# Known mean for layer norm 2, token halves for the first gate/up chunks, late roots on Pool, and a new order of the inverse stage

**Chip, cores, metric.** One core of one Trainium2 chip. The metric is the device time in microseconds (us); the kernel before took 492.64 us (median of 3, 492.58 to 492.88).

## The reference

One transformer-like block over `x` of 2048 tokens by 576 columns, in bfloat16 with float32 inside:

```python
h  = x + irfft2(rfft2(layernorm(x)) * (w_r + 1j*w_i))          # spectral filter
h2 = h + (gelu(layernorm(h) @ w_gate) * (layernorm(h) @ w_up)) @ w_down   # 576 -> 4608 -> 576
```

`layernorm(x)` has mean zero in every token, so the column-frequency-zero part of its spectrum is zero and the filter adds nothing to a token's mean: the mean of `h` is the mean of `x`. The change rests on that.

## The kernel before

Tokens lie in 16 tiles of 128. After the forward transforms, an *inverse stage* makes `h` for tiles 0 to 7, normalises and turns tiles 0 to 3, and then the *body* starts: for each of four blocks of 512 tokens, 36 chunks of gate and up matmuls (two parts each), then the down matmuls. Tiles 8 to 15 are made by deferred inverse work inside the first down phase. The stage's order is written as a string: `I` and `N` are the two inverse matmul steps of a tile, `s` its sum of squares (ScalarE), `m`, `r` statistics (VectorE), `q` square root (ScalarE), `c` reciprocal (VectorE), `n` the normalisation (VectorE; `p` on Pool), `A`, `D`, `z` the turn (a transposition) on TensorE with eviction, the copy out of PSUM, by ScalarE, VectorE or both. In the profiles XO holds the tokens, GS the copy of an `I` result (by ScalarE, on VectorE too for tile 0), HN a normalised tile, HT its turned form, WG and WD the weights. The lines of the code that matter here (`...` marks what is left out):

```python
QR = ((0, 2), (2, 4), (4, NPRE), (NPRE, 16))          # tiles that share one root
SEQ = """I0 I1 N0 I2 s0 N1 I3 N2 m0 s1 I4 r0 q0 s2 N3 c0 m1 s3 n1 n0 r1 I5 q1 N4 I6 A1 c1 n3 A0 n2 N5 I7 D2 z3 N6 N7"""
...
    def st_N(c):                                       # residual add, and the token sums on the side
        ... v.scalar_tensor_tensor(x2, banks(SLOT["N", c], 2, 288), 1.0, x2, op0=ALU.mult, op1=ALU.add,
                                   accum_out=SB2[:, 0, c:c + 1])
    def square(c, out, key):                           # sum of squares
        ... a.activation(out, XO[:, c, 0:D], ACTF.Square, accum_out=SB2[:, 1, c:c + 1])
    def ln2_m(q):  # mean = -sum/D; mean^2             VectorE, two instructions
    def ln2_r(q):  # var = sumsq/D - mean^2            VectorE
    def ln2_q(q):  # sqrt(var + eps)                   ScalarE
    def ln2_c(q):  # 1/sqrt                            VectorE
    def norm(c, eng=DVE):                              # (x - mean) * rs, 576 columns + a repeated 64
...
    for tb in range(4):
        for f in range(36):
            gu_part(36 * tb + f, False)
            if f:
                gu_part(36 * tb + f - 1, True)
            ...
            if tb == 0 and f == 8:
                ln2_m(2); ln2_r(2); ln2_q(2); ln2_c(2)     # tiles 4 to 7
            ...
        if tb == 0:
            ln2_m(3); ln2_r(3); ln2_q(3); ln2_c(3)         # tiles 8 to 15
```

## Time and profile before

| | before |
|---|---|
| traced span | 491.0 us |
| stage start to first gate/up matmul | 48.36 to 60.94, 12.58 us |
| useful TensorE work in it | 10.94 us |
| body, one block: gate/up, down | 70.04, 35.39 us |

The table's second row is the distance from the first `I` matmul of the inverse stage to the first gate/up matmul, both as the chain of waits gives them. The lines are in the prediction.

### The profile page before, as it was taken

What the parts mean: (1) busy time and instruction counts of PE and PEld (TensorE: products, weight loads), DVE (VectorE), ACT (ScalarE), POOL (GpSimd) and SP (SyncE); (2) the same over time, 40 slices, a digit from 0 to 9 for tenths busy, and PEclk for the clock granted to TensorE, in tenths of its full rate; (3) what the DMA queues carried; (4) which work ended last, traced back from release to release, by engine and by line L of the source; (5) the groups of instructions that cost most, each with busy time, mean ns of one, the idle gap of its engine ahead of it and who ended that gap; (6) DMA issues with size and microseconds to landing.
All of it is one profiled execution on the core that took longest, in us unless ns stands there. A gap on an engine that the chain in (4) does not pass through costs nothing.

```text
span 491.0 us, 9838 instructions
## 1 busy us (share of the span) xinstructions
PE 484.6 (99%) x4337; PEld 289.4 (59%) x4338; DVE 195.1 (40%) x416; ACT 155.5 (32%) x296; POOL 24.8 (5%) x41
## 2 busy tenths in 40 slices
PE   7999999999999999999999999999999999999998
PEld 3787655555688844444577644444677544444775
DVE  6999833443456534333311143433211233333111
ACT  6899845323221252232200023223100122333000
POOL 6211601000000010000000000000000000000000
PEclk9999999999999999999999999999999999999999
DMA  8980997210000071100000001000000000000000
GB/s 290 250 309 16 371 365 258 86 28 20 1 13 19 13 232 24 23 3 1 1 19 13 19 16 26 15 1 1 7 19 18 8 2 1 1 1 1 13 19 19
DMA packets 25147, 31.26 MB, mean 64 GB/s; under 512 B 11440, under 2 KB 17840, under 8 KB 25104
## 3 DMA queue, kind: packets, MB, share of 16 engines
q1 hardware_dynamic: 22208, 18.68, 13.0%
q0 software_dynamic: 2896, 11.95, 6.8%
q8 instruction: 34, 0.56, 0.5%
q14 instruction: 9, 0.07, 0.1%
HBM read 26.29 MB, written 2.36 MB: 58 GB/s over the span
## 4 chain that ended last, share of the span: by engine, by line
PE 95%; DVE 2%; DMA 1%; SPq 0%; issue 0%; POOL 0%; DVEq 0%; POOLq 0%
PE PS L841 57%; PE PS L891 29%; PE PS L586 2%; PE PS L596 2%; PE PS L526 1%; DMA XO<-in_A_x_dram 1%; PE PS L626 1%; PE PS L858 1%; PE PS L701 1%; PE PS L740 1%; DVE ST L470 1%; DVE XO L743 0%; PE PS L872 0%; SPq L219 0%; DVE HN L774 0%
## 5 line engine op out<-in xcount | busy, mean ns | idle before, releaser
L841 PE MATMUL PS<-HT,WG 64*128 64x512 bf16 x2106 | 228.5, 376 | 0.0
L841 PEld LDWEIGHTS PS<-HT,WG 64*128 64x128 bf16 x2106 | 107.6, 94 | 119.5 <-issue 1.0
L851 DVE TENSOR_TENSOR AT<-GL,PS 128x512 bf16<-128x512 bf16 x144 | 99.0, 688 | 174.8 <-ACT GL L850 174.8
L850 ACT ACTIVATE GL<-PS 128x512 bf16<-128x512 f32 x144 | 85.9, 597 | 257.2 <-PE PS L841 243.6
L891 PE MATMUL PS<-WD,AT 128*128 128x288 bf16 (+2 forms) x1152 | 144.3, 286 | 0.0
L891 PEld LDWEIGHTS PS<-WD,AT 128*128 128x128 bf16 x1152 | 110.8, 98 | 30.7 <-ACT GL L850 1.3
L894 DVE TENSOR_TENSOR OS<-PS,XO 128x288 bf16<-128x288 f32 (+2 forms) x32 | 14.7, 458 | 100.3 <-PE PS L891 100.3
L841 PE MATMUL PS<-HT,WGX 64*128 64x512 bf16 x486 | 53.4, 376 | 0.0
L841 PEld LDWEIGHTS PS<-HT,WGX 64*128 64x128 bf16 x486 | 23.7, 94 | 28.8
L731 ACT ACTIVATE JD<-XO 128x576 bf16<-128x576 bf16 x8 | 5.5, 683 | 28.5 <-DVE XO L875 28.5
L586 PE MATMUL PS<-FT,U 128*128 128x288 bf16 x96 | 14.2, 286 | 0.0
L605 DVE TENSOR_TENSOR TP<-YS,WS 128x1152 bf16<-128x1152 bf16 (+2 forms) x17 | 11.8, 720 | 0.3
L526 PE MATMUL PS<-ATS,XO 128*128 128x128 bf16 (+1 forms) x128 | 10.1, 221 | 1.3 <-POOL XN L540 0.8
L470 DVE BATCH_NORM_STATS2 ST<-XO 128x6 f32<-128x288 bf16 x24 | 9.3, 439 | 4.1 <-DMA XO<-in_A_x_dram 4.1
L586 PEld LDWEIGHTS PS<-FT,U 128*128 128x128 bf16 x96 | 9.3, 98 | 2.4 <-DVE U L535 0.2
L577 ACT ACTIVATE YS<-PS 128x576 bf16<-128x576 f32 x15 | 9.6, 652 | 2.0 <-PE PS L596 1.8
L774 DVE TENSOR_SCALAR HN<-XO,TM,RS 128x576 bf16<-128x576 bf16 (+1 forms) x32 | 10.0, 363 | 0.0
L596 PE MATMUL PS<-CUS,BT 128*128 128x288 bf16 x64 | 10.0, 286 | 0.0
L526 PEld LDWEIGHTS PS<-ATS,XO 128*128 128x128 bf16 (+1 forms) x128 | 7.5, 97 | 4.0 <-POOL XN L540 1.3
L577 ACT ACTIVATE CUS<-PS 128x576 bf16<-128x576 f32 x14 | 9.1, 651 | 0.8 <-PE PS L586 0.4
L875 DVE SCALAR_TENSOR_TENSOR XO<-PS,XO 128x576 bf16<-128x576 f32 x8 | 6.1, 758 | 8.0 <-PE PS L872 8.0
L626 PE MATMUL PS<-VT,ZS 128*128 128x256 bf16 x64 | 8.8, 273 | 0.3 <-DVE ZS L616 0.3
(79 smaller groups left out, 211.6 us busy)
## 6 DMA issues: line engine op xcount, KB each, us to landing
WD<-in_B_w_down_dram POOLq DMA_DIRECT2D x9, 576.0 KB, 20.8
WG<-in_B_w_up_dram SPq DMA_DIRECT2D x4, 1152.0 KB, 8.1
WG<-in_B_w_gate_dram POOLq DMA_DIRECT2D x4, 1152.0 KB, 10.1
out_dram<-OS SPq DMA_DIRECT2D x30, 72.0 KB, 1.6
XO<-in_A_x_dram SPq DMA_DIRECT2D x3, 576.0 KB, 6.9
WGX<-in_B_w_gate_dram POOLq DMA_DIRECT2D x1, 1152.0 KB, 6.9
WGX<-in_B_w_up_dram SPq DMA_DIRECT2D x1, 1152.0 KB, 10.2
HT<-HN SPq DMA_TRANSPOSE x60, 2.4
```

What stands on the lines that cost most here:

```text
L470: P.op(DVE, lambda v, c=c, h=h: v.bn_stats(ST1[:, c, h, :], XO[:, c, 288 * h:288 * h + 288]), r=[("X", c)], w=[("ST1", c, h)])
L526: P.op(PE, lambda t, b=b, lhs=lhs, p0=p0, p1=p1, s=s, e=e, o=o, c=c: t.matmul(bank(b, p0, p1, o, o + 128), lhs, ATS[:, c, :], start=s, sto ...
L577: fn = (lambda v: v.tensor_copy(dst, src)) if eng == DVE else (lambda a: a.activation(dst, src, ACTF.Copy))
L586: P.op(PE, lambda t, b=b, m=m, us=us, o=o, g=g: t.matmul(bank(b, 0, 128, 0, 2 * HK), U[:, us, g, :, :], FT[:, 3 * o + (2 if us == 4 else u ...
L596: P.op(PE, lambda t, b=b, tb=tb, m=m, s3=s3, sp_=sp_: t.matmul(bank(b, 0, 128, 0, KW), BT[:, sp_, tb, :], CUS[:, s3, m, :], start=(m == 0) ...
L605: P.op(DVE, lambda v: v.tensor_tensor(TP[:, sl, :, :, q0:q1], y4, w4, op=ALU.mult), r=[("Y", sl), ("Wn", i)] + (wkeys[0] if 1 <= g < 9 els ...
L626: P.op(PE, lambda t, b=b[c], c=c, zp=zp, sp_=sp_, z3=z3: t.matmul(bank(b, 0, 128, 256 * c, 256 * c + 256), ZS[:, z3, zp, c:256:2], VT[:, s ...
L841: op = P.op(PE, lambda t, h0=h0, kt=kt, wt=wt, b=b, s=(not second and j == 0), e=(second and j == n - 1): t.matmul(bank(b), wg_tile(slot)[ ...
L850: P.op(ACT, lambda a: a.activation(GL[:, s2, :], bank(b0), ACTF.Gelu_apprx_tanh), r=[("PS", b0)], w=[("GL", s2)])
L851: P.op(DVE, lambda v: v.tensor_tensor(AT[:, f, :], GL[:, s2, :], bank(b0 + 1), op=ALU.mult), r=[("GL", s2), ("PS", b0 + 1)], w=[("AT", f)])
L891: P.op(PE, lambda t, b=b, d0=d0, d1=d1, f=f, p=p: t.matmul(bank(b, 0, 128, 0, d1 - d0), AT[:, f, 128 * p:128 * p + 128], WD[:, f, d0:d1], ...
L894: P.op(DVE, lambda v, b=b, d0=d0, d1=d1, p=p, c=c: v.tensor_tensor(OS[:, p % 2, d0:d1], bank(b, 0, 128, 0, d1 - d0), XO[:, c, d0:d1], op=A ...
```

## The change

Four things at once. (1) The sum of squares is taken around the mean kept from layer norm 1, so the sums, means and mean squares of layer norm 2 go away. (2) The first two chunks run in two token halves, so that the first half needs only tiles 0 and 1 turned. (3) Roots for tiles 4 to 15 become a power of -0.5 on Pool. (4) The stage has a new order, with three of four normalisations on Pool.

```diff
+PARTS = ((0, 256), (256, 512))
-QR = ((0, 2), (2, 4), (4, NPRE), (NPRE, 16))
-SEQ = """I0 I1 N0 I2 s0 N1 I3 N2 m0 s1 I4 r0 q0 s2 N3 c0 m1 s3 n1 n0 r1 I5 q1 N4 I6 A1 c1 n3 A0 n2 N5 I7 D2 z3 N6 N7"""
+QR = ((0, 2), (2, 3), (3, 4), (4, 8), (8, 16))
+SEQ = """I0 I1 N0 I2 s0 N1 I3 s1 N2 I4 q0 s2 c0 N3 I5 s3 p1 q1 N4 q2 I6 N5 c1 c2 p0 A1 I7 n3 N6 A0 z3 N7 p2 D2 G0 G1"""
...
+        P.op(POOL, ... g.tensor_scalar(NM[:, c:c1], src, f, 1.0, ...))        # minus the mean of layer norm 1
-  a.activation(out, XO[:, c, 0:D], ACTF.Square, accum_out=SB2[:, 1, c:c + 1])
+  a.activation(out, XO[:, c, 0:D], ACTF.Square, bias=NM[:, c:c + 1], accum_out=SB2[:, 1, c:c + 1])
-  v.scalar_tensor_tensor(x2, banks(...), 1.0, x2, ..., accum_out=SB2[:, 0, c:c + 1])
+  v.tensor_tensor(x2, banks(...), x2, op=ALU.add)
-  ln2_m, ln2_r
+    def ln2_late(q):
+        P.op(POOL, ... g.tensor_scalar(RS2, SB2[:, 1], 1.0 / D, EPS, op0=ALU.mult, op1=ALU.add))
+        P.op(POOL, ... g.tensor_tensor(RS2, RS2, EXQ, op=ALU.pow))             # EXQ is -0.5
+    def gu_first(i):                                                          # "G0", "G1"
+        for a in range(4):
+            gu_part(a % 2, a > 1, *PARTS[i])
... (PSUM slots of the stage recomputed; deferred work of the first down phase put into a table, same places)
```

More of the change, by code (lines that the diff above doesn't have):

```diff
@@ L28 @@
 DENG, BENG = ['act', 'dve', 'dve', 'act', 'act', 'act', 'act', 'act', 'act', 'act', 'act', 'act', 'act', 'act', 'act', 'act'], ['dve', 'act', 'act', 'act', 'act', 'act', 'act', 'act', 'act', 'act', 'act', 'act', 'act', 'act', 'act', 'act']
-QR = ((0, 2), (2, 4), (4, NPRE), (NPRE, 16))
-SEQ = """I0 I1 N0 I2 s0 N1 I3 N2 m0 s1 I4 r0 q0 s2 N3 c0 m1 s3 n1 n0 r1 I5 q1 N4 I6 A1 c1 n3 A0 n2 N5 I7 D2 z3 N6 N7""".split()
+QR = ((0, 2), (2, 3), (3, 4), (4, 8), (8, 16))
+DSTEP, DLAG = (36, 22) if NPRE == 8 else (28, 22)
+SEQ = """I0 I1 N0 I2 s0 N1 I3 s1 N2 I4 q0 s2 c0 N3 I5 s3 p1 q1 N4 q2 I6 N5 c1 c2 p0 A1 I7 n3 N6 A0 z3 N7 p2 D2 G0 G1""".split()
 def _np_bf16(a):
@@ L355, in _build @@
     EPT = sb.alloc("EPT", [128, 1], F32)
+    EXQ = sb.alloc("EXQ", [128, NT], F32)
+    NM = sb.alloc("NM", [128, NT], F32)
     MK = sb.alloc("MK", [128, 4], F32)
@@ L407, in _build @@
     P.op(POOL, lambda g: g.memset(ZD[:, :], 0.0), w=["ZD"])
+    P.op(POOL, lambda g: g.memset(EXQ[:, :], -0.5), w=["EXQ"])
     P.op(POOL, lambda g: g.memset(MK[:, :], 0.0), w=["MK"])
@@ L548, in _build @@
         RUN1[w[0]](*((int(a[:-1]), ENG[a[-1]]) if a[-1] in ENG else (int(a),)))
+    c = 0
+    while c < NT:
+        c1 = c + 1
+        while c not in ACT_TILES and c1 < NT and c1 not in ACT_TILES:
+            c1 += 1
+        src, f, keys = (SA[:, 0, c:c1], -1.0 / D, "SA0") if c in ACT_TILES else (MV1[:, c:c1, 0], -1.0, "MV1")
+        P.op(POOL, lambda g, c=c, c1=c1, src=src, f=f: g.tensor_scalar(NM[:, c:c1], src, f, 1.0, op0=ALU.mult, op1=ALU.mult),
+             r=[(keys, k) for k in range(c, c1)], w=[("NM", k) for k in range(c, c1)])
+        c = c1
     P.alias([("XN", c) for c in range(NT)], [("V", g, c) for g in range(NG) for c in range(2)])
@@ L690, in _build @@
     vkeys = vk[0] + vk[1] + vk[2]
-    SLOT = {}
-    for w in SEQ:
-        if w[0] in "INADz":
-            SLOT["T" if w[0] in "ADz" else w[0], int(w[1:])] = len(SLOT)
-    SLOT = {k: 2 * ((v - len(SLOT)) % 4) for k, v in SLOT.items()}
+    SLOT, last = {}, [0] * 4
+    smm = [w for w in SEQ if w[0] in "IJNADzG"]
+    g0 = smm.index("G0")
+    for t, w in enumerate(w for w in smm if w[0] != "G"):
+        b = min((2, 3) if t >= g0 - 2 else range(4), key=lambda b: last[b])
+        last[b] = t + 1
+        SLOT["T" if w[0] in "ADz" else "I" if w[0] == "J" else w[0], int(w[1:])] = 2 * b
     def i_mm(c, h, i):
@@ L702, in i_mm, with i_ev @@
                                                               start=(i == 0), stop=(i == 2)), r=vk[i] + ["DT"], w=[("PS", b)])
-    def i_ev(c):
+    def i_ev(c, eng=ACT):
         sl, b0 = c % 2, SLOT["I", c]
@@ L709, in i_ev @@
         else:
-            P.op(ACT, lambda a, sl=sl, b0=b0: a.activation(GS[:, sl, :, 0:KW], banks(b0, 2, KW), ACTF.Copy),
-                 r=[("PS", b0), ("PS", b0 + 1)], w=[("G", sl, 0), ("G", sl, 1)])
+            ev(eng, GS[:, sl, :, 0:KW], banks(b0, 2, KW), [("PS", b0), ("PS", b0 + 1)], [("G", sl, 0), ("G", sl, 1)])
     def st_I01():
@@ L722, in st_I01, with st_I @@
             i_ev(c)
-    def st_I(c):
+    def st_I(c, eng=ACT):
         for h in range(2):
@@ L727, in st_I @@
                 i_mm(c, h, i)
-        i_ev(c)
+        i_ev(c, eng)
     def square(c, out, key):
-        P.op(ACT, lambda a, c=c, out=out: a.activation(out, XO[:, c, 0:D], ACTF.Square, accum_out=SB2[:, 1, c:c + 1]),
-             r=[("X", c)], w=[key, ("S1", c)])
+        P.op(ACT, lambda a, c=c, out=out: a.activation(out, XO[:, c, 0:D], ACTF.Square, bias=NM[:, c:c + 1], accum_out=SB2[:, 1, c:c + 1]),
+             r=[("X", c), ("NM", c)], w=[key, ("S1", c)])
     def st_N(c):
@@ L742, in st_N @@
         x2 = XO[:, c, 0:D].rearrange("p (a b) -> p a b", a=2)
-        P.op(DVE, lambda v, x2=x2, c=c, sl=sl: v.scalar_tensor_tensor(x2, banks(SLOT["N", c], 2, 288), 1.0, x2, op0=ALU.mult, op1=ALU.add,
-                                                               accum_out=SB2[:, 0, c:c + 1]),
-             r=[("PS", SLOT["N", c]), ("PS", SLOT["N", c] + 1)], w=[("X", c), ("S0", c)])
-    def ln2_m(q):
-        c0, c1 = QR[q]
-        P.op(DVE, lambda v, c0=c0, c1=c1: v.tensor_scalar(TM[:, 1, c0:c1], SB2[:, 0, c0:c1], -1.0 / D, None, op0=ALU.mult), r=[("S0", c) for c in range(c0, c1)], w=[("MN", q)])
-        P.op(DVE, lambda v, c0=c0, c1=c1: v.tensor_tensor(TM[:, 0, c0:c1], TM[:, 1, c0:c1], TM[:, 1, c0:c1], op=ALU.mult), r=[("MN", q)], w=[("M2", q)])
-    def ln2_r(q):
-        c0, c1 = QR[q]
-        P.op(DVE, lambda v, c0=c0, c1=c1: v.scalar_tensor_tensor(RS2[:, c0:c1], SB2[:, 1, c0:c1], 1.0 / D, TM[:, 0, c0:c1], op0=ALU.mult, op1=ALU.subtract),
-             r=[("M2", q)] + [("S1", c) for c in range(c0, c1)], w=[("V2", q)])
+        P.op(DVE, lambda v, x2=x2, c=c: v.tensor_tensor(x2, banks(SLOT["N", c], 2, 288), x2, op=ALU.add),
+             r=[("PS", SLOT["N", c]), ("PS", SLOT["N", c] + 1)], w=[("X", c)])
     def ln2_q(q):
         c0, c1 = QR[q]
-        P.op(ACT, lambda a, c0=c0, c1=c1: a.activation(RS2[:, c0:c1], RS2[:, c0:c1], ACTF.Sqrt, bias=EPT[:, 0:1]), r=[("V2", q), "EPT"], w=[("SD2", q)])
+        P.op(ACT, lambda a, c0=c0, c1=c1: a.activation(RS2[:, c0:c1], SB2[:, 1, c0:c1], ACTF.Sqrt, scale=1.0 / D, bias=EPT[:, 0:1]),
+             r=[("S1", c) for c in range(c0, c1)] + ["EPT"], w=[("SD2", q)])
     def ln2_c(q):
@@ L765, in ln2_c @@
         P.op(DVE, lambda v, c0=c0, c1=c1: v.reciprocal(RS2[:, c0:c1], RS2[:, c0:c1]), r=[("SD2", q)], w=[("RS2", q)])
+    def ln2_late(q):
+        c0, c1 = QR[q]
+        P.op(POOL, lambda g: g.tensor_scalar(RS2[:, c0:c1], SB2[:, 1, c0:c1], 1.0 / D, EPS, op0=ALU.mult, op1=ALU.add), r=[("S1", c) for c in range(c0, c1)], w=[("V2", q)])
+        P.op(POOL, lambda g: g.tensor_tensor(RS2[:, c0:c1], RS2[:, c0:c1], EXQ[:, c0:c1], op=ALU.pow), r=["EXQ", ("V2", q)], w=[("RS2", q)])
     def lq(c):
@@ L773, in norm @@
         for i, (o0, o1, x0, x1) in enumerate(((0, D, 0, D), (D, 640, 512, D))):
-            P.op(eng, lambda v, c=c, hs=hs, o0=o0, o1=o1, x0=x0, x1=x1: v.tensor_scalar(HN[:, hs, o0:o1], XO[:, c, x0:x1], TM[:, 1, c:c + 1],
+            P.op(eng, lambda v, c=c, hs=hs, o0=o0, o1=o1, x0=x0, x1=x1: v.tensor_scalar(HN[:, hs, o0:o1], XO[:, c, x0:x1], NM[:, c:c + 1],
                                                                                         RS2[:, c:c + 1], op0=ALU.add, op1=ALU.mult),
-                 r=[("X", c), ("MN", q), ("RS2", q)], w=[("HN", hs, i)])
+                 r=[("X", c), ("NM", c), ("RS2", q)], w=[("HN", hs, i)])
     def turn_dma(c):
@@ L799, in turn_pe, with sq @@
             P.op(e, fn, r=[("PS", b0 + q0 // 512)] + ([("PS", b0 + 1)] if eng else []), w=[("HT", 0, c, k0)])
-    def sq(c):
-        square(c, OS[:, c % 2, :], ("OS", c % 2, 0))
-    RUN = {"I": st_I, "N": st_N, "s": sq, "m": ln2_m, "r": ln2_r, "q": ln2_q, "c": ln2_c, "n": norm, "p": lambda c: norm(c, POOL), "A": lambda c: turn_pe(c, ACT), "D": lambda c: turn_pe(c, DVE),
-           "z": lambda c: turn_pe(c, None)}
-    st_I01()
-    for w in SEQ[2:]:
-        RUN[w[0]](int(w[1:]))
-    P.alias(ukeys + [("CU", a) for a in range(3)], [("WD", j) for j in range(9)])
-    for j in range(9):
-        P.dma(POOL, WD[:, 4 * j:4 * j + 4, :], wdv[:, 4 * j:4 * j + 4, :], f"wd{j}", w=[("WD", j)])
-    P.alias(vkeys, ["EB", "Q0", "Q1", "YB0", "YB1", "JD"])
-    fdead = ["DT", "IT", "J0", "J1", "ZD"] + [(n_, c) for n_ in ("ATB", "ATS") for c in range(NT)] + [("G", 0, 0), ("G", 0, 1), ("G", 1, 0), ("G", 1, 1), ("Y", 0), ("Y", 1)]
-    fdead += [("T", a, h) for a in range(2) for h in range(2)] + [("Z", a) for a in range(NZ)] + [("ZR", a, h) for a in range(2) for h in range(4)]
-    fnew = ([("AT", f) for f in range(36)] + [("GL", 0), ("GL", 1)] + [("HT", 1, i, k) for i in range(4) for k in range(5)])
+    def sq(c, eng=ACT):
+        if eng == ACT:
+            square(c, OS[:, c % 2, :], ("OS", c % 2, 0))
+            return
+        x = XO[:, c, 0:D]
+        P.op(DVE, lambda v: v.scalar_tensor_tensor(OS[:, c % 2, :], x, NM[:, c:c + 1], x, op0=ALU.add, op1=ALU.mult, accum_out=SB2[:, 1, c:c + 1]),
+             r=[("X", c), ("NM", c)], w=[("OS", c % 2, 0), ("S1", c)])
     def fidx(m):
@@ L826, in _build, with gu_part @@
     first_done = {}
-    def gu_part(m, second):
+    def gu_part(m, second, c0=0, c1=512):
         tb, f = m // 36, fidx(m)
@@ L839, in gu_part @@
                 b = 2 * (m % 4) + o
-                aft = [first_done[m, o]] if second and j == 0 else []
+                aft = [first_done[m, o]] if j == 0 and (second or c0) else []
                 op = P.op(PE, lambda t, h0=h0, kt=kt, wt=wt, b=b, s=(not second and j == 0), e=(second and j == n - 1): t.matmul(
-                    bank(b), wg_tile(slot)[h0:h0 + 64, wt, 128 * (f % 9):128 * (f % 9) + 128], HT[h0:h0 + 64, kt, :], start=s, stop=e),
-                    r=[("HT", tb % 2, i, k) for i in range(4) for k in range(5)] + [("WG", slot, i) for i in range(4)],
+                    bank(b, 0, 128, c0, c1), wg_tile(slot)[h0:h0 + 64, wt, 128 * (f % 9):128 * (f % 9) + 128], HT[h0:h0 + 64, kt, c0:c1], start=s, stop=e),
+                    r=[("HT", tb % 2, i, k) for i in range(c0 // 128, c1 // 128) for k in range(5)] + [("WG", slot, i) for i in range(4)],
                     w=[("PS", b)], after=aft)
-                if not second:
-                    first_done[m, o] = op
-        if not second:
+                first_done[m, o] = op
+        if not second or c1 < 512:
             return
@@ L852, in gu_part @@
              r=[("GL", s2), ("PS", b0 + 1)], w=[("AT", f)])
+    def gu_first(i):
+        for a in range(4):
+            gu_part(a % 2, a > 1, *PARTS[i])
+    P.alias([("ATB", c) for c in range(8)], [("AT", 0), ("AT", 1)])
+    RUN = {"I": st_I, "J": lambda c: st_I(c, DVE), "S": lambda c: sq(c, DVE), "N": st_N, "s": sq, "q": ln2_q, "c": ln2_c, "n": norm, "p": lambda c: norm(c, POOL), "A": lambda c: turn_pe(c, ACT), "D": lambda c: turn_pe(c, DVE),
+           "z": lambda c: turn_pe(c, None), "G": gu_first}
+    st_I01()
+    for w in SEQ[2:]:
+        RUN[w[0]](int(w[1:]))
+    P.alias(ukeys + [("CU", a) for a in range(3)], [("WD", j) for j in range(9)])
+    for j in range(9):
+        P.dma(POOL, WD[:, 4 * j:4 * j + 4, :], wdv[:, 4 * j:4 * j + 4, :], f"wd{j}", w=[("WD", j)])
+    P.alias(vkeys, ["EB", "Q0", "Q1", "YB0", "YB1", "JD"])
+    fdead = ["DT", "IT", "J0", "J1", "ZD"] + [(n_, c) for n_ in ("ATB", "ATS") for c in range(NT)] + [("G", 0, 0), ("G", 0, 1), ("G", 1, 0), ("G", 1, 1), ("Y", 0), ("Y", 1)]
+    fdead += [("T", a, h) for a in range(2) for h in range(2)] + [("Z", a) for a in range(NZ)] + [("ZR", a, h) for a in range(2) for h in range(4)]
+    fnew = ([("AT", f) for f in range(2, 36)] + [("GL", 0), ("GL", 1)] + [("HT", 1, i, k) for i in range(4) for k in range(5)])
     def def_i(c):
@@ L874, in def_n, with turn, defer @@
         x2 = XO[:, c, 0:D].rearrange("p (a b) -> p a b", a=2)
-        P.op(DVE, lambda v, x2=x2, c=c: v.scalar_tensor_tensor(x2, banks(4, 2, 288), 1.0, x2, op0=ALU.mult, op1=ALU.add, accum_out=SB2[:, 0, c:c + 1]),
-             r=[("PS", 4), ("PS", 5)], w=[("X", c), ("S0", c)])
+        P.op(DVE, lambda v, x2=x2, c=c: v.tensor_tensor(x2, banks(4, 2, 288), x2, op=ALU.add),
+             r=[("PS", 4), ("PS", 5)], w=[("X", c)])
         square(c, JD[:, :], "JD")
+    def turn(c):
+        norm(c)
+        turn_dma(c)
+    DEF = {}
+    def defer(t, fn, *a):
+        DEF.setdefault(t, []).append(lambda: fn(*a))
+    for j, c in enumerate(range(NPRE, NT)):
+        defer(DSTEP * j, def_i, c)
+        defer(DSTEP * j + DLAG, def_n, c)
+    if NPRE < 8:
+        t2 = DSTEP * (8 - NPRE) + DLAG
+        defer(t2 - 14, ln2_late, 3)
+        for c in range(4, 8):
+            defer(t2 - 2 + DSTEP * (c - 4), turn, c)
     def down(tb, p):
@@ L884, in down @@
             b = (0, 1, 2, 3)[2 * (p % 2) * (tb > 0) + h] if tb or p < 3 else 6 + h
-            cd = NPRE + 2 * p + h if tb == 0 else NT
-            if cd < NT:
-                def_i(cd)
-            for f in [*range(36)] if tb == 0 else [*range(9, 36), *range(9)]:
-                if cd < NT and f == 22:
-                    def_n(cd)
+            for k, f in enumerate([*range(36)] if tb == 0 else [*range(9, 36), *range(9)]):
+                if tb == 0:
+                    for fn in DEF.get(72 * p + 36 * h + k, ()):
+                        fn()
                 P.op(PE, lambda t, b=b, d0=d0, d1=d1, f=f, p=p: t.matmul(bank(b, 0, 128, 0, d1 - d0), AT[:, f, 128 * p:128 * p + 128],
@@ L901, in _build @@
         for f in range(36):
-            gu_part(36 * tb + f, False)
-            if f:
+            if tb or f > 1:
+                gu_part(36 * tb + f, False)
+            if f > 2 or tb and f:
                 gu_part(36 * tb + f - 1, True)
@@ L908, in _build @@
                 sq(4 + f)
-            if tb == 0 and f == 8:
-                ln2_m(2)
-                ln2_r(2)
-                ln2_q(2)
-                ln2_c(2)
+            if tb == 0 and f == 8 and NPRE == 8:
+                ln2_late(3)
             f0, f1 = (15, 3) if tb == 0 else (2, 4)
-            if tb < 3 and f >= f0 and (f - f0) % f1 == 0 and (f - f0) // f1 < 4:
+            if (tb or NPRE == 8) and tb < 3 and f >= f0 and (f - f0) % f1 == 0 and (f - f0) // f1 < 4:
                 norm(4 * (tb + 1) + (f - f0) // f1)
@@ L921, in _build @@
         if tb == 0:
-            ln2_m(3)
-            ln2_r(3)
-            ln2_q(3)
-            ln2_c(3)
+            ln2_late(4)
             P.alias(vkeys + ["DP", "ITD", "EB", "Q0", "Q1", "YB0", "YB1", "JD"], [("WG", 3, k) for k in range(4)])
```

## The prediction

> **What bounds the kernel now.** I read first the chain that ended last, in order of time: it says which engine sets the end, and from when.
>
> ```profile
> 47.35 0.88 DVE VR L641
> 48.23 0.14 issue
> 48.36 1.63 PE PS L701 x12
> ...
> 57.04 0.69 DVE XO L743 x2
> 57.73 0.05 issue
> 57.77 0.66 PE PS L740 x4
> 58.44 0.73 PE PS L701 x6
> 59.17 0.71 PE PS L794 x10
> 59.88 1.02 PE PS L740 x8
> 60.90 0.04 issue
> 60.94 70.11 PE PS L841 x648
> ...
> 172.41 70.04 PE PS L841 x648
> 242.45 35.39 PE PS L891 x288
> ```
>
> Columns: start, length, what. From 60.94 us to the end at 491.0 the chain is TensorE alone, apart from the last 0.4 us: gate and up matmuls (L841), down matmuls (L891) and the deferred inverse between them (41.36 us from 131.05 to 172.41 instead of 35.39). The edit leaves this body as it is but for the first two chunks. So only the start of the body can move: the inverse stage, 48.36 to 60.94, 12.58 us (I matmuls L701, N matmuls L740, turns of the normalised tiles L794).
>
> Second, TensorE's timeline of that stage; the spacing of starts matters, because a matmul's own length (286 ns) overlaps the next.
>
> ```profile
> 55.90 0.29 PE L701 MATMUL PS<-DT,VR 128*128 128x288 bf16 x1
> 56.65 0.91 PE L794 MATMUL PS<-IDT,HN 128*128 128x128 bf16 x10 [0.46 <-DVE HN L774]
> 57.77 0.66 PE L740 MATMUL PS<-GS,IT 128*128 128x288 bf16 x4 [0.21 <-DVE XO L743]
> 59.16 0.72 PE L794 MATMUL PS<-IDT,HN 128*128 128x128 bf16 x10
> 59.74 1.15 PE L740 MATMUL PS<-GS,IT 128*128 128x288 bf16 x8
> 60.94 2.33 PE L841 MATMUL PS<-HT,WG 64*128 64x512 bf16 x20
> ```
>
> Steady spacing is 0.1225 us for a 288-wide matmul (50 from 49.90 to 56.02) and about 0.057 us for a 128-wide turn (ten from 59.16 to 59.74). Work: 80 x 0.1225 + 20 x 0.057 = 10.94 us. The stage lasts 12.58, so TensorE loses 1.64 us: 0.07 before the first N, 0.63 before the first turns (56.02 to 56.65), 0.55 before N5 (57.22 to 57.77), 0.16 at 59.0, 0.22 before L841. This 1.64 us, 0.33% of 492.64, is a ceiling on what a reordering can give.
>
> Third, VectorE and Pool in the same stretch, to see what TensorE waits for.
>
> ```profile
> 53.72 0.48 DVE L751 TENSOR_SCALAR TM<-SB 128x2 f32<-128x2 f32 x1
> 55.79 1.18 DVE L774 TENSOR_SCALAR HN<-XO,TM,RS 128x576 bf16<-128x576 bf16 x4
> 56.95 0.75 DVE L743 SCALAR_TENSOR_TENSOR XO<-PS,XO 128x576 bf16<-128x576 f32 x1
> 59.64 1.16 DVE L798 CAST HT<-PS 128x640 bf16<-128x640 f32 x2
> ```
> ```profile
> 9.43 0.67 POOL L540 TENSOR_SCALAR XN<-XO 128x576 bf16<-128x576 bf16 x1
> 49.71 6.81 POOL L219 DMA_DIRECT2D WD<-in_B_w_down_dram x9
> ```
>
> VectorE runs N-adds, statistics, norms and an eviction in one queue. The N4 add could start at 55.45, when N4's matmuls end, and starts at 56.95 behind statistics and norms; N5 waits for it. L841 starts just after the last turned part leaves PSUM (59.64 + 1.16 = 60.80). Pool only issues the nine WD loads.
>
> **What the Trainium skill says.** "TensorE: Matmul & The Clock Gate", section Back-to-back issue gap, gives N/2.4 + 2.5 ns warm; here 288 columns cost 122.5 ns, which agrees, and a pair of 64-row, 512-wide matmuls 70.04/324 = 216.2 ns, which agrees for two that run side by side. Its section LDWEIGHTS (loading the stationary operand) says a load goes by columns and not by rows: here 94 ns (64 rows) against 98 (128 rows). "SBUF — State Buffer", section Who interferes with whom, says Pool and VectorE's two-port modes lock each other out of a shared port pair; the 128x2 statistics instruction of 0.48 us beside the WD issue, against 0.16 for a 128x4 one at 79.07 with Pool idle, fits. "GPSIMD Engine Reference", section Engine selection, calls one-input work on Pool roughly line rate: the 576-wide XN takes 0.67 us, VectorE's norm 0.43.
>
> **The change part by part.**
>
> *Known mean.* Gone from VectorE in the stage: two L751 (0.48 + 0.31), two L752, two L756 (0.16 each), eight accumulator reads (0.08), together about 2.1 us; added: one more reciprocal, 0.16. Squares now take the mean as bias at the same 0.67 us. The path from the N1 add to a normalised tile shortens to square, root, reciprocal, norm. In the deferred part eight accumulator reads go, beside busy TensorE: worth nothing. Nine tiny Pool instructions (estimated 0.25 us each) make the means after Pool's last XN at 17.1, in a gap that lasts until 24.75: nothing.
>
> *Norms on Pool.* Three of four go there. Estimated from XN: 0.67 for 576 columns, 0.24 for the 64-wide one (864 wide takes 0.91, so 0.83 ns a column on 0.19), about 0.16 between two: 1.2 us a tile. WD issue moves behind them, to about 59 to 66; WD is first read at 131.
>
> *New order.* I placed each instruction with its measured length and queue. N0 to I6 run as before to 56.02, and N5 follows at once: its GS copy ends near 55.9, its bank is free since the N3 add near 55.5. VectorE no longer stands still: N3 add about 54.75, N4 55.5, N5 56.7. ScalarE: root of tiles 0 and 1 at 54.33, reciprocal 54.67 to 54.83. Pool: p1 54.96 to 56.03, p0 to 57.3. TensorE: A1 56.51, I7 56.80, N6 57.6 (0.05 lost for its GS copy), A0 58.08. Reciprocals of tiles 2 and 3 near 57.4, n3 57.65 to 58.25, p2 to 58.75 or 59.0. Then z3 58.37, N7 58.74 (0.09 lost), D2 59.23 to 59.51. Tile 0 leaves PSUM about 59.29, so the first half chunk starts near 59.5 and covers the eviction of D2 (about 60.1 to 60.95). This loses 0.2 instead of 1.64 us. A walk without slips is too good: n3 and p2 want the shared port together, and if Pool wins, z3 and all after it come 0.5 later. I take 59.75 (59.5 to 60.1), a gain of 1.2 us.
>
> *Two token halves.* A chunk has 10 matmuls in its first part and 8 in its second; two chunks are 36 matmuls or 18 pairs of 512 columns, 18 x 216.2 ns = 3.89 us. They become 36 pairs of 256 columns. If streaming binds, 256/2.4 + 2.8 (the surplus of 216.2 over 213.3) = 109.5 ns a pair, 3.94 us; if two loads bind at the 57 ns of a turn with its load, 116 ns, 4.18 us. Cost 0.05 to 0.3, taken as 0.15.
>
> *Roots by Pool.* Four table loads of 1.28 us (78.45, 80.06, 172.33, 174.18) go from ScalarE. TensorE did not wait there (70.11 against 70.04 in the later bodies), so at most 0.07 us. Pool's power has no duration in this trace; for tiles 4 to 7 it has from 78 to the norm at about 91, for the last eight from 172 to 178.
>
> Sum: 1.2 - 0.15 = 1.05 us; 492.64 - 1.05 = 491.6.
>
> **Rivals.** (1) *Pool becomes the wait.* If a norm takes 2 us instead of 1.2, through pointer scalars or lock-out, p2 ends about 61, D2 and the whole body behind it: 492.6 to 493. For: three norms in series on a slow engine in front of D2. Against: the first two have a microsecond of slack. (2) *Weight loads bind in the halves.* At two full 94 ns loads a pair, 36 x 0.188 = 6.8 us, 2.9 more than now: 494.3. Against: turns load 128 columns every 57 ns. (3) *The ceiling is reached*: no port conflict, streaming halves: 60.94 - 59.5 - 0.05 = 1.4, so 491.2. (4) *The power is slow*: at over 6 us the norm of tile 8 blocks VectorE's queue at 178 and gate/up banks fill; a few us lost once. Against: three spare pairs of banks, nearly 6 us of slack.
>
> **Range and chances.** Repeats of before span 0.3 us. The good end is bounded by 1.64; the bad end by rivals 1 and 2, which I hold at one in six together. 491.0 to 492.6. A move of 2% is 9.9 us: six times the idle that exists, and no rival costs it.
>
> **What would show it.** Right: L841 starts at 59.5 to 60.1; 72 matmuls of 64x256 in about 4.0 us; no TensorE wait over 0.3 us after 56; N5 directly behind I6; later bodies still 70.04 and 35.39; ScalarE without root loads after the first body begins. Wrong: a TensorE wait at D2 on Pool's HN, a 256-wide pair over 0.12 us, an L841 start past 60.6, or the first body longer than 70.2 past its halves because VectorE waits for Pool's power.

## The result, and the profile after

| | before | changed |
|---|---|---|
| time, first comparison | 492.76 us (4 runs) | 492.25 us (4 runs), ratio 0.9988, interval 0.9971 to 1.0006 |
| time, five rounds (run `again`) | 492.94 us (9 runs) | 492.19 us (5 runs), ratio 0.9986, interval 0.9973 to 0.9998 |
| traced span | 491.0 us | 490.0 us |
| stage start to body, by the chain | 12.58 us | 11.60 us |
| the same, start to start in the timeline | 12.58 us | 11.54 us |

The times are medians. Ratios are the mean time of one kernel's runs over that of the other's of the same rounds, so not quite the ratio of the medians. The first interval includes 1, the second ends just below it: a gain this small is barely clear of the noise of the times. The prediction was 491.6 (491.0 to 492.6). The time lies in the range, 0.65 us above the point.

The chain that ended last in the changed kernel:

```profile
48.30 1.63 PE PS L717 x12
...
56.13 0.57 PE PS L755 x4
56.70 0.28 PE PS L804 x5
...
58.91 0.57 PE PS L755 x4
59.48 0.42 PE PS L804 x5
59.90 70.08 PE PS L839 x684
...
171.35 70.04 PE PS L839 x648
241.38 35.39 PE PS L926 x288
```

No VectorE piece is left, in the lines left out neither, between the stage's start and the body, where the chain before had several. The body starts at 59.90 instead of 60.94. The later blocks last 70.04 and 35.39 us, as before. The first block has 684 matmuls instead of 648. By the chain it lasts 70.08 instead of 70.11, but 0.07 of that 70.11 is the overlap named above (the piece begins after an idle time). From its first matmul to the first matmul behind it, in the kernel before and in the changed one:

```profile
130.98 0.24 PE L858 MATMUL PS<-DP,V 128*128 128x144 bf16 x1
```
```profile
129.92 0.24 PE L877 MATMUL PS<-DP,V 128*128 128x144 bf16 x1
```

it lasts 70.04 us before (60.94 to 130.98) and 70.08 now (59.84 to 129.92).

TensorE's timeline at the end of the stage (start, length, operation; the I matmuls between are left out):

```profile
56.03 0.66 PE L755 MATMUL PS<-GS,IT 128*128 128x288 bf16 x4
56.53 0.44 PE L804 MATMUL PS<-IDT,HN 128*128 128x128 bf16 x5
...
57.69 0.66 PE L755 MATMUL PS<-GS,IT 128*128 128x288 bf16 x4
58.19 0.72 PE L804 MATMUL PS<-IDT,HN 128*128 128x128 bf16 x10
58.82 0.66 PE L755 MATMUL PS<-GS,IT 128*128 128x288 bf16 x4
59.46 0.44 PE L804 MATMUL PS<-IDT,HN 128*128 128x128 bf16 x5
59.84 6.48 PE L839 MATMUL PS<-HT,WG 64*128 64x256 bf16 x94
```

With the spacings of the prediction (0.1225 us for a 288-wide matmul, 0.057 for a turn), the stage to the first gate/up matmul at 59.84 lasts 11.54 us for 10.94 us of work: 0.6 us lost where before lost 1.64. What remains are small waits: 0.07 before N0, 0.065 before N5, 0.145 before N6 (57.545 to 57.69), 0.06 before N7, 0.15 before D2 (59.31 to 59.46) and 0.095 before the body. Those before N5, N6 and N7 end when ScalarE's copy of an I result is done (55.97, 57.64 and 58.77 in its timeline). D2 comes 0.14 after Pool's last norm is done (59.32). Windows of the stage in the changed kernel, for ScalarE alone (length, busy time, instructions, clock, DMA), split where N5 starts:

```profile
48.30:56.03 7.73, 5.86 (x15) 1.00 1.01 362
56.03:59.84 3.81, 3.79 (x10) 1.00 1.04 350
```

ScalarE is busy 3.79 of the last 3.81 us. Its squares became longer: a bias read per partition takes 769 ns instead of 673 before. "ScalarE: Activation LUTs", section What ACT_TABLE_LOAD costs, of the Trainium skill says this: 186 ns + 0.833 ns a column, and about 93 ns for each pointer operand. The estimate from these figures for 576 columns is 666 and 759 ns, within 10 ns of both measured durations. The prediction had overlooked it.

Pool's timeline, with the norms and then the WD issue, which moved behind them as foreseen:

```profile
54.99 2.73 POOL L784 TENSOR_SCALAR HN<-XO,NM,RS 128x576 bf16<-128x576 bf16 x4 [5.34 <-DVE RS L770]
57.89 1.43 POOL L784 TENSOR_SCALAR HN<-XO,NM,RS 128x576 bf16<-128x576 bf16 x2 [0.17 <-POOL HN L784]
59.26 6.70 POOL L221 DMA_DIRECT2D WD<-in_B_w_down_dram  x9
```

Two tiles take 2.73 and one takes 1.43 us, so 1.4 us a tile. The same timeline in two narrow windows shows the 576-wide instruction of tile 0 (p0) and of tile 2 (p2) alone:

```profile
56.40 0.82 POOL L784 TENSOR_SCALAR HN<-XO,NM,RS 128x576 bf16<-128x576 bf16 x1
```
```profile
57.89 0.94 POOL L784 TENSOR_SCALAR HN<-XO,NM,RS 128x576 bf16<-128x576 bf16 x1 [0.17 <-POOL HN L784]
```

p2's, which began while VectorE's norm n3 ran (57.66 to 58.30), took 0.12 us longer than p0's and p1's (0.82 each).

**The gain in the trace is 1.0 us and the gain in time is 0.5 to 0.75.** Two things lie between.

First, noise from the very start. The first link of every chain is the load of x, and its length varies between executions. The stage starts 42.86 to 42.89 us after the length of that load in all fourteen traces: 5.48 us and 48.36 in before, 5.44 and 48.30 in the changed kernel, 6.14 and 49.02 in the run `tuned` below. So up to 0.7 us of a single run's time has nothing to do with the edit, and versions are best compared by the distance from stage start to body.

Second, each execution's time exceeds its traced span. In before the excess is 1.79 us (mean of the 9 runs beside `again`: 492.93 less 491.13). In the changed kernel it is 2.03 (492.19 less 490.16). So 0.97 us of gain in span gives 0.74 in time, and 0.24 us goes outside the span.

### The profile page after: what moved, and what is told of

Same layout as the page of the kernel before. It is cut to its first block, busy times and chain, and to the rows that moved or that the text cites. A ratio compares the mean times of both kernels' runs of the same rounds, so it can differ in the third digit from the quotient of the medians. Undisturbed runs are those within 1.5% of the kernel's fastest.

```text
span 490.0 us, 9898 instructions
## 1 busy us (share of the span) xinstructions
PE 484.2 (99%) x4373; PEld 285.7 (58%) x4374; DVE 190.9 (39%) x381; ACT 150.9 (31%) x291; POOL 33.4 (7%) x61
## 4 chain that ended last, share of the span: by engine, by line
PE 96%; DVE 1%; DMA 1%; SPq 0%; POOL 0%; issue 0%; POOLq 0%; DVEq 0%
PE PS L839 57%; PE PS L926 29%; PE PS L600 2%; PE PS L610 2%; PE PS L531 1%; PE PS L717 1%; DMA XO<-in_A_x_dram 1%; PE PS L640 1%; PE PS L755 1%; PE PS L877 1%; DVE ST L475 1%; PE PS L891 0%; PE PS L804 0%; SPq L221 0%; DVE VR L655 0%; DVE TP L619 0%
## 5 line engine op out<-in xcount | busy, mean ns | idle before, releaser
L839 PE MATMUL PS<-HT,WG 64*128 64x512 bf16 (+1 forms) x2142 | 228.5, 373 | 0.0
L839 PEld LDWEIGHTS PS<-HT,WG 64*128 64x128 bf16 x2142 | 104.1, 94 | 122.7 <-issue 0.7
L746 ACT ACTIVATE JD<-XO,NM 128x576 bf16<-128x576 bf16 x8 | 6.2, 776 | 28.4 <-DVE XO L894 28.4
L894 DVE TENSOR_TENSOR XO<-PS,XO 128x576 bf16<-128x576 f32 x8 | 6.1, 758 | 8.0 <-PE PS L891 8.0
L591 ACT ACTIVATE V<-PS 128x512 bf16<-128x512 f32 (+1 forms) x17 | 9.0, 582 | 0.0
```

The source lines that it names most:

```text
L591: fn = (lambda v: v.tensor_copy(dst, src)) if eng == DVE else (lambda a: a.activation(dst, src, ACTF.Copy))
L839: op = P.op(PE, lambda t, h0=h0, kt=kt, wt=wt, b=b, s=(not second and j == 0), e=(second and j == n - 1): t.matmul(bank(b, 0, 128, c0, c1) ...
```

## The experiments

All kernels were correct. Twelve ran, with five rounds each. They ran in four groups (the first four of the table after before, the next three, then dvenorm2 to poolroots, then the last two); each group shared one chip and the nine runs of before on it. "Stage" is the distance from stage start to body, by the chain and from start to start in the timeline. It comes from one trace a run; where the stage was the same, traces agree within 0.02 us (12.56 to 12.58, 11.60 to 11.61). The means of the times are less certain: the intervals reach about 0.6 us to each side, so only `dvenorm` differs from before clearly, and `again` and `whole` just so.

| run | stage by the chain, us | stage, start to start, us | mean time less mean of before beside it, us | time less span, mean, us |
|---|---|---|---|---|
| before | 12.58 | 12.58 | 0 | 1.77 to 1.80 |
| again (changed) | 11.60 | 11.53 | -0.74 | 2.03 |
| whole | 12.85 | 12.85 | +0.60 | 2.02 |
| dvenorm | 13.34 | 13.27 | +0.96 | 2.03 |
| actroot | 11.61 | 11.54 | -0.33 | 2.14 |
| old_halves | 12.30 | 12.23 | -0.13 | 1.95 |
| old_whole | 12.34 | 12.34 | +0.17 | 2.01 |
| tuned | 12.01 | 11.94 | 0.00 | 2.18 |
| dvenorm2 | 12.19 | 12.12 | -0.15 | 2.08 |
| padpool | 12.56 | 12.56 | +0.26 | 1.78 |
| poolroots | 12.56 | 12.56 | +0.51 | 2.17 |
| tuned2 | 11.61 | 11.54 | -0.55 | 2.20 |
| tuned3 | 11.62 | 11.56 | -0.45 | 2.21 |

**The change again (`again`).** No edit.

> The changed kernel unaltered, five rounds, to size the gain: its trace put the first gate/up matmul 1.0 us earlier after the stage's start (11.54 us instead of 12.58) and the span 1.0 us shorter, the four timed pairs only 0.5 us. Theory A (the trace is right, the timed runs were noisy): 0.8 to 1.1 us faster, 491.6 to 491.9. Theory B (something outside the trace's span gives half of it back): 0.4 to 0.6 us faster, and span again shorter by 1.0.

The measured 0.74 us (492.19 against 492.93, means) lies between the two theories. The spans show why: 0.97 us shorter in the mean, and the excess over the span 0.24 larger. Theory B holds for a quarter of the gain.

**New order with whole chunks (`whole`).**

```diff
-PARTS = ((0, 256), (256, 512))
+PARTS = ((0, 512),)
-... p2 D2 G0 G1
+... p2 D2 G0
```

> Changed kernel, but the first two chunks whole (512 tokens) at the end of the new order. Theory A (order and halves earn the gain together, because the new order leaves the last turn for the end and only a half chunk can cover its eviction): the first gate/up matmul waits for VectorE's eviction of tile 2, which ended at 61.01 in the trace of the changed kernel, so it starts near 61.1, 1.2 us later than with halves, and the time is 0.2 us above before or equal to it. Rival C (the known mean alone earns the gain by emptying VectorE's queue): the start stays near 60.0 and the time 0.5 to 1 us under before.

TensorE's timeline in this run has the foreseen wait, by name:

```profile
59.73 0.44 PE L804 MATMUL PS<-IDT,HN 128*128 128x128 bf16 x5
61.42 2.77 PE L839 MATMUL PS<-HT,WG 64*128 64x512 bf16 x24 [1.25 <-DVE HT L808]
```

Stage 12.85 us (12.8 expected): by the chain 1.25 longer than with halves, and 0.27 longer than before the change. The new order without the halves is a loss. The time rose by 0.60 us, more than the 0.2 expected: 0.37 of it is span and 0.23 is excess over the span.

**Old order, halves and whole (`old_halves`, `old_whole`).** Both keep the known mean and the roots on Pool.

```diff
-SEQ = (new order)
+SEQ = """I0 I1 N0 I2 s0 N1 I3 N2 s1 I4 q0 s2 N3 c0 s3 n1 n0 I5 q1 q2 N4 I6 A1 c1 c2 n3 A0 n2 N5 I7 D2 z3 N6 N7 G0 G1"""
 (old_whole: PARTS = ((0, 512),), and no G1)
```

> Changed kernel with the old order of the inverse stage (all norms on VectorE, turns of tiles 1 and 0 between I6 and N5, of 2 and 3 before N6), known mean and halves kept. Theory A (new order and halves earn the gain only together): VectorE's statistics are gone, so the 0.63 and 0.55 us waits before the first turns and N5 shrink but do not vanish; halves gain only the 0.2 us wait before the first gate/up matmul. Body starts 0.3 to 0.7 us after the changed kernel's (11.9 to 12.2 us from the stage's start). Rival C (the known mean alone is the gain): same start as the changed kernel, 11.5.

> Old order, whole chunks, known mean kept: what the known mean gives alone. Theory A: 12.1 to 12.5 us from the stage's start to the first gate/up matmul (before: 12.58, changed: 11.54), so 0.1 to 0.5 us of the gain. Rival C: 11.6 to 11.7.

Stages of 12.30 (just above the 11.9 to 12.2 expected) and 12.34. The chain's 12.30 has the overlap in it and 12.34 has not, so here the starts are compared. The known mean with the old order gives 0.24 us (12.58 less 12.34), and the halves take 0.11 more from the stage. With `whole` and `again` this makes a square, from start to start: old order 12.34 whole and 12.23 in halves; new order 12.85 whole and 11.53 in halves. The new order alone costs 0.51, the halves alone save 0.11, both together save 0.81 (each time less the 0.04 that the halves cost in the first block). Rival C is out: the gain is neither the mean's alone nor that of either other part alone. No run has the new order and the halves without the known mean, so what the mean adds to those two is not known. The new order puts a turn directly in front of the body, and only a chunk that can start without it pays for that.

**All norms on VectorE (`dvenorm`, `dvenorm2`).**

```diff
 dvenorm:  p1, p0, p2 -> n1, n0, n2 in place
 dvenorm2: ... N3 I5 s3 n1 q1 N4 n0 q2 I6 N5 c1 c2 A1 I7 n3 n2 N6 A0 z3 N7 D2 G0 G1
```

> Changed kernel with all norms of the first four tiles on VectorE, same places in the order. If the three Pool norms are worth their 1.4 us each: n0 and n3 then run one after the other behind N5's add (two times 0.6), z3 comes 0.5 us later and the body starts near 60.3 to 60.5, 0.4 to 0.6 later than with Pool. If Pool's p2 is the wait that binds (D2 stood 0.15 behind it): the body starts at 59.7 or earlier.

The first form missed: stage 13.34, not 12.0 to 12.2. I had left n2 behind N7's add in VectorE's queue, a place that costs nothing on Pool's queue and 1.40 us here, by TensorE's wait at D2.

> A fair form of the run with all norms on VectorE: there n2 stood behind N7's add in the queue, which I had overlooked; here each norm stands at the earliest place that its root allows. Theory (Pool's norms pay, because VectorE's queue is full at the end of the stage): n3, n2 and N6's add in a row put D2 at about 60.0 and the body at about 60.3, 0.4 to 0.6 us after the changed kernel's (12.0 to 12.2 us from the stage's start; changed 11.60). Rival: Pool's norms bring nothing or cost, start at 11.6 or earlier.

Stage 12.19, 0.59 us longer than with Pool. VectorE's timeline shows the queue (two norms, then N6's add, which must leave its PSUM bank before D2 can write there), and TensorE's the wait that follows:

```profile
58.09 1.19 DVE L784 TENSOR_SCALAR HN<-XO,NM,RS 128x576 bf16<-128x576 bf16 x4
59.18 0.75 DVE L758 TENSOR_TENSOR XO<-PS,XO 128x576 bf16<-128x576 f32 x1
```
```profile
59.99 0.45 PE L804 MATMUL PS<-IDT,HN 128*128 128x128 bf16 x5 [0.19 <-DVE XO L758]
```

Pool is over twice as slow at a norm (1.4 us against 0.6) and still the right place for three of them.

**Late roots (`actroot`, `poolroots`).** The first undoes that part alone in the changed kernel, the second does it alone in the kernel before.

```diff
 actroot:    ln2_late(3) -> ln2_q(3); ln2_c(3)      and the same for 4
 poolroots:  before, ln2_q(2); ln2_c(2) -> add eps, pow on Pool      and the same for 3
```

> Changed kernel with the roots of tiles 4 to 15 by ScalarE's Sqrt and VectorE's reciprocal again, so the four table loads of 1.28 us come back. Theory: they lie beside busy TensorE; no change of time (within 0.1 us of the changed kernel), first body at most 0.05 longer. Rival: the loads delay gelu and PSUM banks: 1 to 3 us slower.

> The kernel before with only the roots of tiles 4 to 15 moved to Pool's power; four table loads go. Theory: they lay beside busy TensorE; the bodies stay 70.1 and 70.04, time unchanged (within 0.15 us). Rival: roots by Pool are part of the gain, 0.3 us or more faster. Time minus span tells whether the power instruction makes the 0.2 us outside (2.0) or not (1.8).

Bodies and stages did not move: 11.61 us and a first block of 70.08 in `actroot` with its table loads, 12.56 and 70.11 in `poolroots` without them. On TensorE's path the roots' engine is worth nothing. By time, `actroot` is 0.41 us slower than `again` and `poolroots` 0.51 slower than before, which contradicts the letter of both expectations, though neither is clear of the intervals. Of the 0.41, 0.30 is span, with a load of 5.79 us in the trace against 5.43; 0.11 is excess. Of the 0.51, 0.12 is span and 0.39 is excess over the span; that mean comes from two of its five executions, at 2.49 and 2.53, while the other three lie at 1.93 to 1.95. The power takes 1.04 us for 128x4 and 1.65 us for 128x8, in `poolroots` and in the changed kernel alike. Both are far inside the 6 us and more that they had.

**The added set-up alone (`padpool`).** The kernel before plus the -0.5 memset and the nine mean instructions, unused.

> The kernel before plus the added Pool set-up alone (the -0.5 memset and the nine mean instructions, their results unused). In every variant of the changed kernel the time exceeded the traced span by 1.95 to 2.2 us, in before by 1.8: about 0.2 us of the gain lies outside the span. If the extra Pool instructions make it: 2.0 here, and the time 0.2 us above before. If not: 1.8, time as before (within 0.1 us).

The excess stayed at 1.78 us, so these instructions don't make it. (The time, 0.26 us above before, missed the 0.1 expected; all of it is span, with a load of 5.88 us in the trace against 5.48.) `poolroots` has the memset and the power and shows 2.17, but `actroot` has no power and shows 2.14. **What makes 0.2 to 0.4 us outside the span stays open**: it is steady in some kernels (1.74 to 1.86 in all 9 runs of before beside `again`; 2.12 to 2.16 in the 5 of `actroot`), not in others (1.90 to 2.12 in `old_halves`, 1.93 to 2.53 in `poolroots`), its mean differs between kernels, and no part tried here accounts for it.

**Three other orders (`tuned`, `tuned2`, `tuned3`).**

```diff
 tuned:   ... N3 I5 s3 p1 N4 n0 I6 q1 q2 N5 c1 c2 A1 I7 n3 N6 A0 z3 N7 p2 D2 G0 G1
 tuned2:  ... N2 J4 q0 s2 c0 N3 I5 s3 p1 q1 q2 N4 I6 c1 c2 N5 p0 A1 I7 n3 N6 A0 z3 N7 p2 D2 G0 G1    (J: copy by VectorE)
 tuned3:  ... N2 J4 q0 s2 c0 N3 I5 s3 p1 N4 I6 q1 q2 N5 c1 c2 p0 A1 I7 n3 N6 A0 z3 N7 p2 D2 G0 G1
```

> New order mended where the trace of the changed kernel still shows waits: the norm of tile 0 goes to VectorE's gap after the N4 add, so Pool makes two norms instead of three and p2 no longer holds D2 (0.15 us), and the two single-tile roots come after I6's copy on ScalarE, so N6 no longer waits for it (0.15 us). If these are the waits: first gate/up matmul 0.2 to 0.3 us earlier than in the changed kernel, 11.25 to 11.35 us from the stage's start; timed 0.2 to 0.3 us faster. If ScalarE's queue as a whole binds: no earlier than 11.5.

> ScalarE was busy 3.79 of the last 3.81 us before the body in the changed kernel, and four of TensorE's six small waits there were for its copies. Here the copy of I4 goes to VectorE, into the 0.98 us in which it waited for the first root, and the late roots and reciprocals come earlier. If ScalarE's queue is what is left: body 0.2 to 0.3 us earlier, 11.25 to 11.4 us from the stage's start (changed 11.60 by the chain). Rival (Pool and VectorE meet at the shared port, as in the first tuned order): p2 starts before n3, n3 takes about 1.0 instead of 0.64, z3 comes late, body at 11.6 or later. Span against the changed kernel's only where the input load is the same length; time minus span may differ by 0.2 either way.

> As tuned2, but roots and reciprocals of tiles 2 and 3 stay late (after I6's copy and N5's add), so p2 waits behind p0 until after n3 has taken the port. If both theories hold: n3 at 0.64 us, no wait of N6 for ScalarE's copy, body at 11.3 to 11.5 us from the stage's start. If Pool's three norms bind D2 alone: 11.5 to 11.6, no gain over the changed kernel.

None is earlier: 12.01, 11.61 and 11.62 by the chain. The waits they were made for did go. N6 in `tuned2` follows I7 with no gap. In their place stands one wait that the prediction had named. VectorE's (its two instructions in two windows), Pool's and TensorE's timelines of `tuned2`:

```profile
58.01 0.42 DVE L784 TENSOR_SCALAR HN<-XO,NM,RS 128x576 bf16<-128x576 bf16 x1
```
```profile
58.35 0.73 DVE L784 TENSOR_SCALAR HN<-XO,NM,RS 128x64 bf16<-128x64 bf16 x1
```
```profile
58.10 0.95 POOL L784 TENSOR_SCALAR HN<-XO,NM,RS 128x576 bf16<-128x576 bf16 x1 [0.17 <-DVE XO L758]
```
```profile
59.23 0.44 PE L804 MATMUL PS<-IDT,HN 128*128 128x128 bf16 x5 [0.30 <-DVE HN L784]
```

The norm n3, 0.64 us in the changed kernel (57.66, just before Pool's p2 at 57.89), takes 1.09, 1.07 and 0.99 us in the three orders, where the two begin within 0.12 us of each other, and the turn z3 waits for it. This fits "SBUF — State Buffer", section Who interferes with whom, of the skill: who issues first has the shared ports for a whole instruction, and the other waits. In `tuned` Pool's p2 started first (58.47 against 58.59), and VectorE's 576-wide instruction took 0.87 us instead of 0.43. In `tuned2` VectorE started first (58.01 against 58.10) and in `tuned3` both at 58.19, and the norm still took 1.0 us. The single instructions show how: the 576-wide one kept its 0.42, but the 64-wide one took 0.73 instead of 0.29 and ended 0.04 us after Pool's 576-wide one (59.08 against 59.05); in `tuned3` 0.65 and again 0.04 after. So Pool came between the norm's two instructions. In the changed kernel the 64-wide one kept its 0.29 us, although p2 had begun before it (57.89 against 58.00); why is not shown. In `tuned` n3 also began later, 9.57 us after the stage's start against 9.36 in the changed kernel, behind the late reciprocals. No version here beats the changed kernel.

## Why the prediction was right, point by point

- **The bound.** Right: only the start of the body moved. The later blocks have the same lengths to 0.01 us. (The chain itself ends at 489.08 us; the last 1.9 us to 491.0 lie behind it, not in "the last 0.4".)
- **Ceiling and gain.** The stage was to shrink by 1.2 us; it shrank by 1.04 (12.58 to 11.54). The ceiling of 1.64 held.
- **Known mean.** Right in kind: VectorE's queue emptied, and N5 followed I6 after 0.065 us, nearly as walked (at once). Alone it gives 0.24 us (`old_whole`). The mean instructions on Pool took 0.19 to 0.21 us each, not 0.25.
- **Norms on Pool.** Mis-sized: 1.2 us a tile predicted, 1.4 measured. Without VectorE's norm beside it the 576-wide instruction took 0.82 us instead of 0.67, and the 64-wide one 0.39 instead of 0.24. A norm reads two scalars per partition, and the estimate came from an instruction with constants; that this is the cause is likely, but no run separates it. p2 ended at 59.32 instead of 58.75 to 59.0, and D2 stood 0.15 behind it. So one of the listed signs of being wrong did appear, a wait at D2 on Pool's HN, in a small form of rival 1.
- **Squares.** Wrong: "at the same 0.67 us"; they took 0.77. They stand before the copies in ScalarE's queue, which has no gap from 51.81 on. The waits before N5, N6 and N7 were 0, 0.05 and 0.09 us in the walk and are 0.065, 0.145 and 0.06, so 0.27 instead of 0.14. That the squares make this difference is argued from the queue; no run tested it alone.
- **Port conflict.** The estimate allowed 0.25 for it. In the changed kernel it spared n3 (0.64 us) and z3, but p2 took 0.12 us longer beside n3, which is most of D2's 0.15; in the three tuned orders it held up n3.
- **Halves.** Mis-sized on the safe side: 0.15 us predicted, 0.04 measured (70.08 less 70.04). The first block holds 306 pairs of 512 columns at 216.2 ns, 66.16 us; the other 3.92 of its 70.08 are 36 pairs of 256, so 109 ns a pair, against 109.5 worked out for streaming. Rival 2 is out.
- **Roots.** Right that they lie beside busy TensorE. The 0.07 us of the first block (70.11 against 70.04), which the prediction put down as the most that they could cost, is no time at all but the chain's way of counting; from start to start both are 70.04, and `poolroots`, without table loads for roots in the body, has 70.11 by the chain too.
- **The sum.** 1.05 us predicted; 1.0 in span in the trace, 0.5 and 0.74 in time. That the span came so close is partly luck: the stage gave 1.04 instead of 1.2, the halves cost 0.04 instead of 0.15, and the two errors cancel. The term that was missing is the excess of the time over the span, 1.8 us before and 2.03 after, which I had not thought could change; what changes it is open.

## What to carry to other kernels

Where TensorE is 99% busy, add up its work in the one stretch where it is not: the difference to the stretch's length is the ceiling of any reordering, here 1.64 us of 492. Two changes can be worth little or less than nothing alone and most of the gain together (halves 0.11 us, order a loss of 0.51, both 0.81), so try pairs before dropping either. And measure changes of under 1 us from a point behind the input load, from start to start: the load moved the time by up to 0.7 us by itself.

## What the Trainium skill lacked or had wrong

- "TensorE: Matmul & The Clock Gate", section Back-to-back issue gap: it calls about 81 ns the sustained spacing for 128 columns with a weight load each, in a real kernel. The turns here load weights for each matmul and start every 55 ns (57 counted up to the next matmul of another kind), and 288 columns every 122.5 ns, as its formula for an isolated matmul says.
- The same page has no figure for two 64-row matmuls side by side at 256 columns: 109 ns a pair, with both weight loads hidden (216.2 ns at 512).
- "GPSIMD Engine Reference" gives no cost of scalars read per partition on Pool: a two-scalar instruction of 576 bfloat16 columns took 0.82 us undisturbed against 0.67 with constants, one of 64 columns 0.39 us.
- The same page has no power: 1.04 us for 128x4 and 1.65 us for 128x8 in float32.
- "SBUF — State Buffer", section Who interferes with whom, says who waits at the shared port but not how much it costs when a norm on VectorE is made of two instructions: 1.0 to 1.1 us instead of 0.64 beside a norm on Pool, also where VectorE started first, because its second instruction then waited for Pool's.
- No page gives the excess of a kernel's time over the span from its first to its last instruction, or says that it depends on the kernel: here 1.8 us for the kernel before, 1.95 to 2.2 for the changed kernel and its variants. The gap that "Runtime: NRT & Kernel Launch" has is one between other quantities.
